# Strided heads' transposes moved into the second layer, batch 1's strided heads first, and the last output tile in halves

## The chip, the cores and the metric

The kernel runs on one core of a Trainium2 chip. A core has a matrix engine (TensorE, PE in the profile), a vector engine (VectorE, DVE), an activation engine (ScalarE, ACT), GpSimd (POOL) and SyncE (SP); the last two issue nearly all transfers here, which run on 16 shared DMA engines. TensorE's results go to PSUM, eight banks of 2 KB per partition, and are copied from there by DVE or ACT. The metric is the device time of one execution in microseconds, the median over runs.

## The reference

Two stages follow each other. The first is attention over 8 batches, 8 heads, 576 positions and a head size of 64. Heads 0 to 3 look at the last 32 positions, heads 4 to 7 at every fourth of the last 128:

```python
scores = scale * np.matmul(q, k.transpose(0, 1, 3, 2))
rel = pos[:, None] - pos[None, :]
mask_plain = (rel >= 0) & (rel < window)                # window 32
mask_dil = (rel >= 0) & (rel < window * dilation) & (rel % dilation == 0)   # dilation 4
scores = np.where(masks, scores, -1e9)
attn = exp(scores - max); attn = attn / (sum(attn) + 1e-9)
attn_out = np.matmul(attn, v)
```

The second is a two-layer network on the 4608 tokens (8 x 576) of 512 features, the heads side by side:

```python
h = x @ w_in                        # 512 -> 2048
g = h * (1.0 / (1.0 + np.exp(-h)))  # Silu
out = g @ w_out                     # 2048 -> 512, float32
```

## The kernel before

All matmuls are in float16 with sums in float32. The work of one batch has three parts.

Attention is done in two halves that the code calls z: z = 0 is the four plain heads, z = 1 the four strided heads, whose positions are sorted into four residue classes. One half of one batch goes through these steps:

- `load_qk` brings Q and K with positions on the partitions (tiles `n0`, `n1`; POOL issues the loads, eight per batch).
- `transpose` turns K (`which` = 1) or Q (0) on TensorE into two PSUM tiles `t`, 36 small transposes each for z = 0 and 12 each for z = 1; two copies bring them to SBUF, the first on DVE, the second on ACT (line 264 into `kT` and `qT`, line 273 into `kC` and `qC`). `transposes` does K and then Q.
- `scores` makes the score matmuls of 32 queries by 64 keys into PSUM tiles `s` and `ss` (72 matmuls for z = 0, 80 for z = 1), adds the mask on DVE (lines 414 and 423, tile `ms`) and takes the negative maximum (line 430, `nm`).
- `exps` runs Exp on ACT, one instruction per 64 keys with the maximum as bias and the sum taken out (line 458, 18 or 20 instructions per half). For batch 1's strided heads `shift` subtracts the maximum on DVE first (line 440), so that ACT needs one wide instruction per tile (line 452), and DVE makes the sums later (line 467).
- `normal` divides by the sums on DVE (lines 471 to 474, tile `pn`), `turn` transposes the result on TensorE (line 483), `turned` copies it out on DVE (line 491, `ptT`).
- `values` multiplies with V (lines 516, 570, 581; tiles `x`, `xs`), and `finish` copies the result on DVE into `xT`, the input of the network.

The first layer runs over 16 blocks f of the 2048 features: eight matmuls into a PSUM tile `h` (line 610) and a Silu on ACT into `gT` (line 618). Batch 0's first layer is done in two parts of the positions, two blocks at a time (lines 629 and 636). The second layer takes output tiles of 128 tokens, four for an even batch and five for an odd one (two batches make nine): 16 matmuls each (line 646) into a PSUM tile `o`, a copy on DVE into `ob` (line 654) and a transfer to the output by SP (line 656).

Exp and Silu are in different tables of ACT, which changes between them by a table load, once at the start of each first layer and once at its end.

PSUM is shared out as two tiles of two banks (`big`, for `h` and `o`) and four tiles of one bank (`ps`, for all else, given out in turn); a tile is free again when its copies are done.

The order of the work is written out by hand, and every engine keeps it. The main loop goes through the batches; for each, the first layer and then the second. Before each piece `plan(s)` puts out what `plan_of(b)` has listed for step s. Steps 0 to 15 are the blocks of the first layer, and from 16 on each step is four matmuls of the second layer, so 16 to 31 for an even batch and 16 to 35 for an odd one. For batch 0 the first part of the first layer has steps -16 to -1. Within one batch's first and second layer the plan thus places the attention of the next batch: scores of the plain heads in the second layer of the batch before the last, scores of the strided heads at step 9 of the first layer, exps at step 16, and the rest (`later`) at four given steps.

Of the kernel before, what the change touches and what calls it, by code (L numbers as in the profile page):

```python
# [14 lines left out]
P = 128  # L15
# [12 lines left out]
def kernel(  # L28
# [9 lines left out]
    nc = tc.nc  # L38
    B, H, S, D = q.shape
    DM, DFF = moe_w_in.shape  # L40
# [146 lines left out]
    def clear_v(b, engine):  # L187
# [13 lines left out]
        out=band[0:W], in_=band[0:W], compare_op=ALU.is_ge, fill=NEG,  # L201
# [3 lines left out]
        out=band[0:W], in_=band[0:W], compare_op=ALU.is_ge, fill=NEG,  # L205
# [432 lines left out]
    def layer2(b, plan):  # L638

        tiles = range(0, 4) if b % 2 == 0 else range(4, 9)  # L640
        for x, t in enumerate(tiles):
            o = big.tile([P, 2, 512], F32, tag="big", name=f"o_{b}_{t}")[:, 0]
            for f in range(NFF):
                if f % 4 == 0:
                    plan(NFF + 4 * x + f // 4)
                nc.tensor.matmul(  # L646
                    o,
                    gT[:, f, t * P : (t + 1) * P],
                    w_out16[:, f, :],
                    start=(f == 0),  # L650
                    stop=(f == NFF - 1),
                )
            ob = o32.tile([P, DM], F32, tag="o32", name=f"ob_{b}_{t}")
            nc.vector.tensor_copy(ob, o)  # L654
            row = (b // 2) * 2 * S + t * P
            nc.sync.dma_start(out=out[row : row + P, :], in_=ob)

    both = (nc.vector.tensor_copy, nc.scalar.copy)  # L660

    def transposes(at, b, z, step):
        for which in (1, 0):
            at(step, transpose, b, z, which, both)

    def later(at, b, z, steps):

        for hi in (0, 1):
            at(steps[hi], normal, b, z, hi)
        for fn in (turn, turned):  # L670
            for hi in (0, 1):
                at(steps[2], fn, b, z, hi)
        at(steps[3], values, b, z)
        at(steps[3], finish, b, z)

    def plan_of(b):
        ev = {}

        def at(s, fn, *args):
            ev.setdefault(s, []).append((fn, args))  # L680

        def all_exps(b, z):
            for hi in (0, 1):
                at(16, exps, b, z, hi)

        if b == 0:

            at(-15, normal, 0, 1, 1)
            at(-14, turn, 0, 1, 1)
            at(-14, turned, 0, 1, 1)  # L690
            at(-13, normal, 0, 0, 1)
            at(-12, values0, 1, 1)
            at(-12, finish0, 1, 1)
            at(-10, turn, 0, 0, 1)
            at(-10, turned, 0, 0, 1)
            at(-8, last_values, 0, 1, 1)
            at(-8, last_finish, 0, 1, 1)
            at(-7, values0, 0, 1)
            at(-7, finish0, 0, 1)
            at(-3, last_values, 0, 0, 1)  # L700
            at(-3, last_finish, 0, 0, 1)
            transposes(at, 1, 0, 1)
            at(5, scores, 1, 0)
            transposes(at, 1, 1, 8)
            at(10, load_qk, 3)
            at(10, load_v, 2)
            at(10, shift_v, 2, nc.gpsimd, (ALL,))
            at(12, scores, 1, 1)
            for hi in (0, 1):
                at(12, shift, 1, 1, hi)  # L710
            at(14, shift_v, 1, nc.sync, (ALL,))
            all_exps(1, 0)
            all_exps(1, 1)
            later(at, 1, 0, (20, 22, 25, 26))
            later(at, 1, 1, (25, 27, 29, 30))
        elif b == 1:
            at(16, load_v, 3)
            at(16, shift_v, 3, nc.gpsimd, (ALL,))
            transposes(at, 2, 0, 2)
            transposes(at, 2, 1, 9)  # L720
            transposes(at, 3, 0, 15)
            at(6, scores, 2, 0)
            at(17, load_qk, 4)
            at(12, scores, 2, 1)
            all_exps(2, 0)
            all_exps(2, 1)
            at(17, scores, 3, 0)
            at(18, exps, 3, 0, 0)
            at(18, exps, 3, 0, 1)
            later(at, 2, 0, (22, 24, 27, 28))  # L730
            later(at, 2, 1, (29, 31, 33, 34))
        else:
            if b + 2 < B:
                at(16, load_v, b + 2)
                at(16, shift_v, b + 2, nc.gpsimd, (ALL,))
            if b + 1 < B:
                transposes(at, b + 1, 1, 0)
                later(at, b + 1, 0, (0, 0, 4, 6))
                if b + 3 < B:
                    at(16, load_qk, b + 3)  # L740
            if b + 2 < B:
                transposes(at, b + 2, 0, 13)
                at(17, scores, b + 2, 0)
                at(18, exps, b + 2, 0, 0)
                at(18, exps, b + 2, 0, 1)
            if b + 1 < B:
                at(9, scores, b + 1, 1)
                all_exps(b + 1, 1)
                later(at, b + 1, 1, (22, 24, 27, 28))

        def plan(s):
            for fn, args in ev.pop(s, ()):
                fn(*args)

        return plan
# [36 lines left out]
    for b in range(B):  # L792
        plan = plan_of(b)
        if b == 0:
            for part in (0, 1):
                for f in range(0, NFF, 2):
                    plan(f - NFF * (1 - part))
                    plan(f - NFF * (1 - part) + 1)
                    layer1_part(f, part)
        else:  # L800
            for f in range(NFF):
                plan(f)
                layer1(b, f)
        layer2(b, plan)
        for s in range(NFF, 3 * NFF):
            plan(s)
# [30 lines left out]
```

## Time and profile before

| what | value |
|---|---|
| median of 3 runs | 343.28 us (342.47 to 344.01) |
| profiled execution, its own time | 343.56 us |
| span of its instructions | 341.8 us |
| mean granted TensorE clock | 0.993 |
| busy: TensorE, ACT, DVE, POOL | 314.5, 216.6, 180.5, 88.3 us |
| second layer, line 646 | 576 matmuls, 129.5 us |
| first layer, line 610 (batches 1 to 7) | 896 matmuls, 115.9 us |
| first layer of batch 0, line 629 | 128 matmuls, 20.8 us |

The span is from the first to the last instruction; the execution's own time has 1.8 us around it. Batch 0's first layer begins at 25.8 us and its second at 53.4, batch 1's first layer at 74.1 and its second at 94.1. From there two batches take about 77 us. The last matmul ends at 338.1 us.

How to read the lines that follow: in a row by time the columns are start, length (both us), engine, line, operation, the tile written and the tiles read, shapes, and how many instructions are merged; a bracket says how long the engine sat idle before it and what ended that. PEld is TensorE's loading of weights, which overlaps its matmuls. In a list of waits the numbers are the total in us, how often, and the longest. The granted clock is a share of TensorE's full speed.

### The profile page before, as it was taken

To read this page: it belongs to the slowest core of one execution; us is meant where nothing else is said; L and a number is where in the kernel's file an instruction comes from. 1 tells how busy PE (TensorE), PEld (TensorE's weight loads), DVE (VectorE), ACT (ScalarE), POOL (GpSimd) and SP (SyncE) were. 2 spreads that over 40 slices of the span, in tenths; PEclk is the share of its full clock that TensorE was granted. 3 is DMA by queue.
4 is the path that set the end of the run, shared out by engine and by line. 5 is a ranking of instruction groups with operands and counts; after the bars stand their busy time and mean duration, and the time that the engine had idled before them with its cause. 6 is when DMAs were issued, how large, how long until landed. Compare 5 with 4: busy or idle time off the path is not lost.

```text
span 341.8 us, 11965 instructions
## 1 busy us (share of the span) xinstructions
PE 314.5 (92%) x5216; PEld 204.4 (60%) x5216; DVE 180.5 (53%) x382; ACT 216.6 (63%) x746; POOL 88.3 (26%) x148
## 2 busy tenths in 40 slices
PE   4549799789999899998999899998999899999995
PEld 3437565457745577457755587457755577457642
DVE  7776337765658725765555535665556533440011
ACT  2693548516699856976699456976699456916400
POOL 8825746352500560047003530042000000000000
PEclk9999989999999999999999999999999999999999
DMA  6999999977802894079502980066002100110021
GB/s 83 166 219 205 193 195 213 210 136 100 133 22 82 125 138 78 35 118 172 79 28 80 190 134 2 34 117 115 2 17 80 63 2 2 61 63 2 0 86 70
DMA packets 45061, 32.90 MB, mean 96 GB/s; under 512 B 21872, under 2 KB 39536, under 8 KB 45008
## 3 DMA queue, kind: packets, MB, share of 16 engines
q0 software_dynamic: 38816, 21.74, 46.4%
q1 hardware_dynamic: 6192, 10.39, 8.6%
q8 instruction: 41, 0.67, 0.8%
q14 instruction: 12, 0.10, 0.1%
HBM read 37.75 MB, written 9.44 MB: 138 GB/s over the span
## 4 chain that ended last, share of the span: by engine, by line
PE 78%; ACT 9%; DMA 5%; DVE 3%; issue 2%; POOL 1%; SPq 0%; POOLq 0%
PE o L646 31%; PE h L610 30%; PE h L629 6%; ACT pe L458 4%; PE t L260 3%; PE x L516 2%; PE pt L483 2%; DMA vw<-in_v_dram 2%; ACT L618 2%; DMA vw<-vw 2%; DMA n<-in_k_dram 2%; PE s L306 1%; PE s L318 1%; DVE pn L474 1%; ACT gT L618 1%
## 5 line engine op out<-in xcount | busy, mean ns | idle before, releaser
L646 PE MATMUL o<-w_out,gT 128*128 128x512 f16 x576 | 129.5, 380 | 0.0
L610 PE MATMUL h<-xT,w_in 128*128 128x288 f16 x896 | 115.9, 287 | 4.5 <-ACT gT L618 4.5
L618 ACT ACTIVATE gT<-h 128x576 f16<-128x576 f32 x112 | 72.3, 650 | 64.3 <-PE h L610 63.5
L610 PEld LDWEIGHTS <-w_in 128*128 128x128 f16 x896 | 85.3, 98 | 27.5 <-issue 5.4
L458 ACT ACTIVATE pe<-ms,nm 128x64 f32<-128x64 f32 x284 | 94.3, 334 | 3.3 <-DVE nm L387 3.2
L646 PEld LDWEIGHTS <-gT 128*128 128x128 f16 x576 | 54.7, 98 | 61.7
L654 DVE COPY ob<-o 128x512 f32<-128x512 f32 x36 | 24.8, 689 | 61.2 <-PE o L646 61.2
L458 ACT ACTIVATION_READ_ACCUMULATOR pe<-ms,nm 128x1 f32 x284 | 53.2, 187 | 0.0
L414 DVE SCALAR_TENSOR_TENSOR ms<-s,mask 128x512 f32<-128x512 f32 x28 | 19.2, 686 | 40.3 <-PE ss L306 19.3
L127 POOL DMA_DIRECT2D vw<-in_v_dram x16 | 10.0, 630 | 94.0 <-PE x L516 94.0
L474 DVE TENSOR_TENSOR pn<-pe,r 128x640 f16<-128x640 f32 (+2 forms) x32 | 25.3, 792 | 1.1
L597 DVE CAST xT<-x 128x512 f16<-128x512 f32 x28 | 18.0, 685 | 12.0 <-PE xs L570 10.3
L430 DVE TENSOR_REDUCE nm<-ms 128x10 f32<-128x640 f32 (+1 forms) x28 | 22.0, 786 | 1.0
L629 PE MATMUL h<-xT,w_in 128*128 128x256 f16 (+1 forms) x128 | 20.8, 322 | 0.8 <-DVE xT L556 0.8
L491 DVE COPY ptT<-pt 128x640 f16<-128x640 f16 (+2 forms) x32 | 13.9, 469 | 13.8 <-PE pt L483 13.6
L636 ACT ACTIVATE gT<-h 128x512 f16<-128x512 f32 (+1 forms) x16 | 10.4, 650 | 15.5 <-PE h L629 15.4
L102 POOL DMA_DIRECT2D n<-in_q_dram x28 | 16.4, 598 | 12.5 <-DMA w_in<-in_moe_w_in_dram 6.4
L102 POOL DMA_DIRECT2D n<-in_k_dram x28 | 16.4, 594 | 11.4 <-DMA w_in<-in_moe_w_in_dram 3.9
L483 PE MATMUL pt<-ident,pn 128*128 128x128 f16 x152 | 12.7, 228 | 4.7 <-DVE pn L474 4.7
L629 PEld LDWEIGHTS <-w_in 128*128 128x128 f16 x128 | 13.2, 108 | 5.5 <-issue 0.8
L483 PEld LDWEIGHTS <-pn 128*128 128x128 f16 x152 | 10.4, 101 | 8.0 <-DVE pn L474 5.3
L273 ACT COPY kC<-t 128x576 f16<-128x576 f16 x7 | 4.5, 637 | 15.4 <-PE t L260 15.4
(79 smaller groups left out, 252.7 us busy)
## 6 DMA issues: line engine op xcount, KB each, us to landing
out_dram<-ob SPq DMA_DIRECT2D x36, 256.0 KB, 2.0
n<-in_k_dram POOLq DMA_DIRECT2D x28, 144.0 KB, 5.4
n<-in_q_dram POOLq DMA_DIRECT2D x28, 144.0 KB, 5.6
vw<-in_v_dram POOLq DMA_DIRECT2D x8, 288.0 KB, 6.2
vw<-in_v_dram POOLq DMA_DIRECT2D x16, 128.0 KB, 4.1
w_in<-in_moe_w_in_dram POOLq DMA_DIRECT2D x4, 512.0 KB, 11.6
w_out<-in_moe_w_out_dram POOLq DMA_DIRECT2D x4, 512.0 KB, 10.6
vw<-vw POOLq DMA_DIRECT2D x12, 128.0 KB, 3.3
```

Source lines behind the costliest of these rows:

```text
L102: nc.gpsimd.dma_start(out=qk[b, z, which][i * HF : i * HF + UPS[z]].rearrange("p h u d -> p h (u d)"), in_=src[b, h : h + 2].rearrange("h ...
L414: nc.vector.scalar_tensor_tensor(out=ms[:, 0:8].rearrange("p (n t) c -> p n (t c)", n=2), in0=s[hi].rearrange("p n t c -> p n (t c)"), sca ...
L430: nc.vector.tensor_reduce(out=nm[:, 0:w], in_=ms[:, 0:w], axis=AX.X, op=ALU.max, negate=True)
L458: nc.scalar.activation(pe[:, t, :], ms[:, t, :], AF.Exp, bias=nm[:, t : t + 1], accum_out=l[:, t : t + 1],)
L474: nc.vector.tensor_tensor(pn[:, 0:w], a["pe", z, hi][:, 0:w], r[:, 0:w, None].broadcast_to([P, w, KB]), ALU.mult)
L483: nc.tensor.transpose(t[:, i, :], a["pn", z, hi][:, 2 * i : 2 * i + 2].rearrange("p t c -> p (t c)"), ident)
L597: copy(a["xT"][:, 2 * z : 2 * z + 2, 0:NS].rearrange("d n (m e c) -> d n m e c", e=2, c=run)[:, :, :, e, :], a["x", z][e].rearrange("d n ( ...
L610: nc.tensor.matmul(h[:, half, 0:HS], w_in16[:, c, f * P : f * P + P], xT[:, c, half * HS : half * HS + HS], start=(c == 0), stop=(c == MC ...
L618: nc.scalar.activation(gT[:, f, s0 : s0 + S].rearrange("p (a c) -> p a c", a=2), h[:, :, 0:HS], AF.Silu)
L629: nc.tensor.matmul(h[:, i, 0 : c1 - c0], w_in16[:, c, (f + i) * P : (f + i + 1) * P], xT[:, c, c0:c1], start=(c == 0), stop=(c == MC - 1),)
L646: nc.tensor.matmul(o, gT[:, f, t * P : (t + 1) * P], w_out16[:, f, :], start=(f == 0), stop=(f == NFF - 1),)
L654: nc.vector.tensor_copy(ob, o)
```

## The change

Three things are changed in the order of the work, and nothing in what is computed.

The strided heads' transposes for batches 4 to 7 went out at step 0, ahead of a first layer. They now go out at step 30 of the second layer before it. Those for batch 3 went out at step 0 of batch 2 too; now K's go out at step 1 and Q's at step 3 of batch 2.

For batch 1, prepared during batch 0, the two halves change places. Strided heads: transposes at step -2 (before 8), scores and `shift` at 4 (before 12), `later` at 18, 20, 25, 26 (before 25, 27, 29, 30). Plain heads: transposes at 8 (before 1), scores at 14 (before 5), `later` at 22, 25, 28, 29 (before 20, 22, 25, 26). The exps of the strided heads now come first.

The very last output tile is copied and sent in two halves of 256 columns: the first copied by ACT and sent from ACT's queue, the second copied by DVE and sent from SP's. Before, DVE copied all 512 columns and SP sent them.

```diff
             ob = o32.tile([P, DM], F32, tag="o32", name=f"ob_{b}_{t}")
-            nc.vector.tensor_copy(ob, o)
             row = (b // 2) * 2 * S + t * P
-            nc.sync.dma_start(out=out[row : row + P, :], in_=ob)
+            if (b, t) == (B - 1, 8):
+                m = DM // 2
+                nc.scalar.copy(ob[:, 0:m], o[:, 0:m])
+                nc.scalar.dma_start(out=out[row : row + P, 0:m], in_=ob[:, 0:m])
+                nc.vector.tensor_copy(ob[:, m:DM], o[:, m:DM])
+                nc.sync.dma_start(out=out[row : row + P, m:DM], in_=ob[:, m:DM])
+            else:
+                nc.vector.tensor_copy(ob, o)
+                nc.sync.dma_start(out=out[row : row + P, :], in_=ob)
...
-            transposes(at, 1, 0, 1)
-            at(5, scores, 1, 0)
-            transposes(at, 1, 1, 8)
+            transposes(at, 1, 1, -2)
+            at(4, scores, 1, 1)
+            for hi in (0, 1):
+                at(4, shift, 1, 1, hi)
+            transposes(at, 1, 0, 8)
...
-            at(12, scores, 1, 1)
-            for hi in (0, 1):
-                at(12, shift, 1, 1, hi)
+            at(14, scores, 1, 0)
             at(14, shift_v, 1, nc.sync, (ALL,))
+            all_exps(1, 1)
             all_exps(1, 0)
-            all_exps(1, 1)
-            later(at, 1, 0, (20, 22, 25, 26))
-            later(at, 1, 1, (25, 27, 29, 30))
+            later(at, 1, 1, (18, 20, 25, 26))
+            later(at, 1, 0, (22, 25, 28, 29))
...
             if b + 1 < B:
-                transposes(at, b + 1, 1, 0)
+                if b == 2:
+                    for n in (0, 1):
+                        at(1 + 2 * n, transpose, 3, 1, 1 - n, both)
                 later(at, b + 1, 0, (0, 0, 4, 6))
...
+            if b + 2 < B:
+                transposes(at, b + 2, 1, 30)
```

## The prediction

> **What bounds the kernel now.** I read the busy table first, then the chain of waits, then who waited for whom on TensorE, then the order in time around each wait found.
>
> ```profile
> span 341.8 us, 11965 instructions
> PE 314.5 (92%) x5216; PEld 204.4 (60%) x5216; DVE 180.5 (53%) x382; ACT 216.6 (63%) x746; POOL 88.3 (26%) x148
> ...
> PE 78%; ACT 9%; DMA 5%; DVE 3%; issue 2%; POOL 1%; SPq 0%; POOLq 0%
> ```
> ```profile
> PE pt L483 <- DVE pn L474: 4.7, 4, 1.8
> PE h L610 <- ACT gT L618: 4.5, 5, 0.9
> PE s L306 <- issue: 2.4, 1, 2.4
> ```
>
> TensorE (PE) bounds it: 92% busy and 78% of the chain. Its work is only reordered, so time can come only from its waits. After the start (matmuls of the first layer from 25.8 us) these are, in order: 2.37 us at 40.8 put down to issue; 1.51 and 1.82 us in batch 0's second layer, for `pn` from VectorE (DVE); five of 0.90 us for ScalarE (ACT); 0.33 at 299.1.
>
> ```profile
> 152.00 0.77 PE L260 MATMUL t<-ident,n 48*128 48x48 f16 x48
> ...
> 152.54 0.64 ACT L273 COPY kC<-t 128x576 f16<-128x576 f16 x1 [1.94 <-PE t L260]
> ...
> 153.07 0.65 ACT L273 COPY qC<-t 128x576 f16<-128x576 f16 x1
> ...
> 153.74 1.28 ACT L618 ACT_TABLE_LOAD   x1
> ...
> 155.03 1.19 ACT L618 ACTIVATE gT<-h 128x576 f16<-128x576 f32 x2
> ...
> 155.73 2.12 PE L610 MATMUL h<-xT,w_in 128*128 128x288 f16 x16 [0.90 <-ACT gT L618]
> ```
>
> This is the start of batch 3, and those of batches 2, 4, 5 and 6 look the same. ACT had nothing to do for 1.94 us, then got two copies, and only then loaded the Silu table; TensorE, with two `h` buffers, ran out of them.
>
> ```profile
> 43.15 0.19 PE L306 MATMUL s<-kT,qT 64*32 64x64 f16 x1 [2.37 <-issue]
> ```
> ```profile
> 43.00:44.00 1.00, 0.85 (x9) 0.58 (x9) 0.62 (x2) 0.00 (x0) 0.00 (x0) 0.83 1.24 206
> 44.00:45.00 1.00, 1.00 (x6) 0.56 (x4) 0.97 (x3) 0.00 (x0) 0.56 (x1) 0.50 1.32 197
> ...
> 46.00:47.00 1.00, 1.00 (x5) 0.56 (x4) 0.00 (x0) 0.10 (x1) 0.00 (x0) 0.50 1.96 168
> 47.00:48.00 1.00, 1.00 (x51) 0.68 (x49) 0.21 (x1) 0.61 (x2) 0.50 (x1) 0.96 2.26 173
> ```
> ```profile
> q8 instruction: 1, 0.02, 5.5%
> ```
>
> Columns of the middle lines: stretch, its length, busy time of PE, PE's weight loads, DVE, ACT, POOL, then granted clock, DMA share, GB/s. The gap comes five score matmuls before the end of `scores(1, 0)`; then the clock is 0.5 until about 47.1. The 16 matmuls after the gap take 4.02 us where equal ones take 2.35: another 1.67 lost. The last line is DMA between 40.8 and 41.9 us: a 16 KB instruction packet, started at 40.87, done at 41.84; 1.31 us later TensorE goes on. There are 41 such packets for about 10,450 TensorE instructions, one per 256. Counting from the gap back, the previous boundary was crossed at 37.2; so the packet lay 3.6 us in full queues (DMA is over 90% busy until 60 us). The neighbours agree: crossed 43.15 and started 47.24, crossed 50.6 and started 54.35. Later, with emptier queues, a packet starts within 1 us and is at least 3.5 us early.
>
> **The change part by part.** The sum is made against the profiled execution, 343.56 us (span 341.8 and 1.8 around it); the median of the three runs, 343.28, is 0.28 below.
>
> *Starts of batches 2 to 6.* For batches 3 to 6 the 48 transposes and their four copies go to step 30 of the second layer before. Take the one at 152: step 30 lies 8 matmuls (1.7 us) before its end, so transposes at about 150.3. Exps hold ACT until 150.6; then 0.64 + 0.65 for `kC` and `qC` to 152.1, and the table load of 1.28 to 153.4. The first `h` still starts at 152.7 (transposes merely come earlier) and is done at 153.75: the table is there 0.35 before it is wanted. After odd batches there are 5 us instead of 1.7. Buffers at step 30: the four `ps` tiles were last `x` and `xs`, copied out by 149.65 and 149.91. DVE now has `kC`, `qC` (0.75 each, to 152.1) before `ob`, which is ready at 152.7 anyway; the normals behind end earlier than before. Batch 2's start instead gets batch 3's transposes after `h` 0 and `h` 2: ACT has 0.33 us free per `h` (0.65 of 0.98), so each copy (0.64) delays one Silu by 0.3, which two buffers absorb; DVE does the normals (2.3 us) first, `kC` by 3.7 and `qC` by 4.9 after the start, turns come at 5. So 5 x 0.90 = 4.5 go. Cutting one more run of matmuls costs TensorE about 0.1 (24 `h` matmuls between two switches 3.05, 24 of an unbroken run 2.94), six times, 0.5 rounded: **-4.0**. Bounds: -4.5 (switches free) and -2.5 (ACT late by half the stall after each).
>
> *Batch 1's order in the first layer of batch 0.* Transposes (48 at step -2, 72 at step 8), scores (80 at 4, 72 at 14) and copies are the same ones, next to the same matmuls; the strided K and Q of batch 1 were issued at 15.4 to 17.6 us, and the slowest such load takes 15.5, so they are there at 36.1. DVE's `shift` now follows the first scores: 5.2 us of work from 41 to 46.2; the plain transposes' copies behind it (2 x 0.75) end at 47.7, wanted by `scores(1, 0)` at 48.0. What does move is the count of instructions. The boundary crossed at 37.2 is now crossed in the transposes about 0.6 earlier (36.7), so its block is there at 36.7 + 3.6 + 1.0 + 1.3 = 42.6. The next boundary falls, by the order of the built program, no longer inside the scores but three matmuls into `h` of f = 6, reached at 42.5: a wait of 0.15 in place of 2.37, too short for the clock row to repeat (the 1.82 gap at 68 left it at 1.00). The block after that, asked for at 42.65 with 4.1 of queue, is there at 49.0 and wanted in `scores(1, 0)` at 48.4: 0.6 of new wait (before, the slow clock hid it). So 2.37 + 1.67 - 0.75 = 3.3, less 0.1 for one more switch: **-3.2**. Bounds: -4.0 (no fetch wait left) and +1.0 (old wait and clock loss stay, and the 0.6 - 1.0 comes on top). I take the row-based value because three packets agree on 3.6 to 4.1.
>
> The Trainium skill, "TensorE: Matmul & The Clock Gate", Part 1, speaks against the clock part: it has the clock fall only after an idle window of about 3.4 us. Here 2.37 us were enough; by the page that 1.67 would not belong to the gap and this term would be -1.5, the sum 1.7 less.
>
> *Batch 0's second layer.* It starts at L (53.36 before) and takes 20.75 to the next `h` at 74.11. Now: ACT's table is there at L+2.2, two shifted exps (0.67 each) to 3.5, 18 plain ones (0.33) to 9.5. DVE in its order: normal 2.1 to L+5.1; `ob` 0.69 to 5.8; normal to 7.9; plain normal 1.2 to 9.1; `ob` to 9.8; both `ptT` 0.9 to 10.7; the last normal to 11.9; finish 1.65 to 13.55. TensorE turns at 7.95, does 4 matmuls to 9.5, then values wait for `ptT` until 10.75: 1.25 us, new. `ob` 14.45, `ptT` 15.3, values at 15.35: 0.05. The two `pn` waits (1.51 + 1.82) go, since `pn` is there 0 and 1.8 early. 3.33 - 1.3, less 0.1: **-1.9**. Bounds: -3.2 and -0.5 (DVE 0.7 later at each of the two turns). On POOL nothing is moved; SP's four moves of V for batch 1 keep their place (landed by 56.3).
>
> *Last tile.* The 0.69 copy becomes 0.4 on ACT (between 128x256 f16 at 0.372 and Silu of 512 at 0.600) and 0.42 on DVE (128x256 CAST). In the built program the DVE half waits for the ACT half, so data is out at about 0.87: 0.18 later. The last transfer moves 0.8 us for 256 KB (packets 339.6 to 340.4); half of it saves up to 0.4, and ACT's half is away before. ACT has no queued work then. **-0.1**, between -0.4 and +0.4.
>
> The Trainium skill, "PSUM — Partial Sum Buffer", on bank collisions, says why: two engines may not touch one bank and quadrant at once, so halves of one bank go in turn. Had they run together, by the rows 0.27 would be saved instead of 0.18 lost.
>
> Sum: -4.0 - 3.2 - 1.9 - 0.1 = -9.2, so **334.4 us**.
>
> **The rivals.** (1) The fetch wait stays: if the block comes no earlier, or the next one starves `scores(1, 0)` for over 2 us, the half clock follows again. For it: no profile shows that queue at 36.7, and the margin is tenths. The term goes from -3.2 to about 0: 337.6. (2) ACT is not freed: at step 30 it is late after the even batches (2 of 5 starts, margin 0.35), or the turn after `h` 3 of batch 2 waits. Then up to 2.0 of the 4.0 stay: 336.4. (3) Slower: the step-30 transposes wait for DVE's finish copies, in the middle of the bound engine's stream, four times. They have 0.25 to 0.5 us of margin and DVE sat idle 0.93 before the like finish at 113.25, which speaks against it; it would have to cost (9.2 + 1.7)/4 = 2.7 us at each for a loss of 0.5%, say 346. (4) The change does nothing that counts: a later wait in each first layer takes back the 0.90 and the fetch wait stays; 341 to 343. Against it: no other TensorE wait of those batches is in the trace, and pn is ready about 1 us before its turn.
>
> **How the numbers follow.** Forecast 0.62 (332.8 to 336 by its own bounds), rival 1 0.18, rival 2 0.10, rival 3 0.04, rival 4 0.06. Under 0.5%, 1.7 us, a measurement of this kernel can't tell from no change (the runs shown spread over 1.5). Rivals 1 and 2 together reach 339.5, so 332.5 to 339.5 leaves out rivals 3 and 4 and some of the edges, under 0.2. Faster is the forecast, 1, 2 and a little of 4: 0.90; same most of 4: 0.05; slower 0.05.
>
> **What would show it.** Right: no `PE h L610 <- ACT gT L618` wait and the table load ahead of the first `h`; an issue gap under 1 us near 42 and 48 with the clock at 1.00; one wait `x <- ptT` of about 1.2 in place of two for `pn`; the stretch from the first `h` of batch 1 on shorter by 4. Wrong: the clock at 0.5 anywhere after 26 us, waits of `t L260` for DVE, or DVE's half copy waiting long at the end.

## The result and the profile after

| what | before | after |
|---|---|---|
| median of 4 runs each | 343.33 us (342.47 to 344.01) | 333.95 us (332.95 to 334.36) |
| ratio of the times | | 0.9724, 95% interval 0.9693 to 0.9754 |
| profiled execution | 343.56 us, span 341.8 | 332.95 us, span 331.2 |
| mean granted clock | 0.993 | 1.000 |

The changed kernel is 2.8% faster: 9.4 us by the medians, 10.6 by the two profiled executions. The one of after is the lowest of its four runs, which accounts for the 1 us between the two figures.

The page of after, its span, its busy table and the engines' shares of the chain that ended last:

```profile
span 331.2 us, 11975 instructions
...
PE 312.4 (94%) x5216; PEld 204.4 (62%) x5216; DVE 181.0 (55%) x382; ACT 217.4 (66%) x747; POOL 88.2 (27%) x148
...
PE 85%; DMA 4%; DVE 3%; ACT 3%; POOL 2%; issue 2%; SPq 0%; POOLq 0%; ACTq 0%
```

TensorE has the same 5216 matmuls and is busy 2.1 us less, most of it because the stretch at half clock is gone. Its share of the chain rises from 78 to 85%, and ACT's falls from 9 to 3%. From the list of who waited for whom on TensorE in after (total in us, how often, longest):

```profile
PE pt L483 <- DVE pn L474: 1.7, 2, 1.3
...
PE x L516 <- DVE ptT L491: 0.7, 2, 0.5
PE s L306 <- issue: 0.7, 1, 0.7
...
PE x L516 <- issue: 0.5, 1, 0.5
```

There is no line `h L610 <- ACT gT L618` any more; before it had 4.5 us in five waits. Of the four waits for `pn`, 4.7 us, two are left: one lies ahead of the change's first step and the other, 0.33 us, near 289. The new ones in order of time, from the timeline of TensorE:

```profile
48.57 0.49 PE L306 MATMUL s<-kT,qT 64*32 64x64 f16 x42 [0.71 <-issue]
```
```profile
60.02 0.19 PE L516 MATMUL x<-ptT,vw 64*64 64x32 f16 x1 [0.51 <-DVE ptT L491]
60.41 0.70 PE L516 MATMUL x<-ptT,vw 64*64 64x32 f16 x63 [0.21 <-DVE ptT L491]
65.89 0.30 PE L516 MATMUL x<-ptT,vw 64*64 64x32 f16 x14 [0.51 <-issue]
```

The start of batch 3, the counterpart of the stretch at 152 shown for before:

```profile
144.10 0.77 PE L260 MATMUL t<-ident,n 48*128 48x48 f16 x48
...
144.64 0.64 ACT L273 COPY kC<-t 128x576 f16<-128x576 f16 x1 [0.22 <-PE t L260]
...
145.17 0.65 ACT L273 COPY qC<-t 128x576 f16<-128x576 f16 x1
...
145.84 1.28 ACT L618 ACT_TABLE_LOAD   x1
...
146.54 1.51 PE L610 MATMUL h<-xT,w_in 128*128 128x288 f16 x11
...
147.72 0.65 ACT L618 ACTIVATE gT<-h 128x576 f16<-128x576 f32 x1 [0.60 <-PE h L610]
```

The last bracket has turned round: ACT now waits 0.60 us for TensorE's `h`, where TensorE had waited 0.90 us for ACT.

To see where the time went, I cut the span of each profiled execution in four, at instructions that every kernel has: A, from the span's start to the 49th `h` matmul of batch 0 (a bit before the first step that the change touches); B, from there to the first `h` of batch 1 (the rest of batch 0's two layers); C, from there to the end of the last matmul; D, what follows it.

| kernel | A | B | C | D |
|---|---|---|---|---|
| before | 35.16 | 38.95 | 263.93 | 3.74 |
| after | 35.33 | 33.45 | 258.87 | 3.53 |
| difference | +0.17 | -5.50 | -5.06 | -0.21 |

B splits at the start of batch 0's second layer into 18.20 + 20.75 before and 14.82 + 18.63 after: -3.38 and -2.12. A holds nothing that was changed; over the profiled executions below it takes 34.4 to 36.8 us, and 37.3 in experiment 4, so single times differ by a microsecond or two without any cause in the change, and B and C are what to compare. Most of that spread goes with the clock, though its column reads 1.00 there. In after, eight first-layer matmuls of batch 0 take at first as long as sixteen do later:

```profile
27.80 1.91 PE L629 MATMUL h<-xT,w_in 128*128 128x256 f16 x8
...
33.31 1.92 PE L629 MATMUL h<-xT,w_in 128*128 128x256 f16 x16
```

The rate doubles at 30.8 us, where the trace's record of the clock begins; the column counts the time ahead of that record as full. In the three executions where this comes earliest, at 28.4 to 28.9 us, A is 34.4 to 34.7; in the four where it comes latest, at 32.2 to 33.1, A is 36.6 to 37.3.

### The profile page after: what moved, and what is told of

Same layout as the page of the kernel before. It is cut to its first block, busy times and chain, and to the rows that moved or that the text cites. A ratio compares the mean times of both kernels' runs of the same rounds, so it can differ in the third digit from the quotient of the medians.

```text
span 331.2 us, 11975 instructions
## 1 busy us (share of the span) xinstructions
PE 312.4 (94%) x5216; PEld 204.4 (62%) x5216; DVE 181.0 (55%) x382; ACT 217.4 (66%) x747; POOL 88.2 (27%) x148
## 4 chain that ended last, share of the span: by engine, by line
PE 85%; DMA 4%; DVE 3%; ACT 3%; POOL 2%; issue 2%; SPq 0%; POOLq 0%; ACTq 0%
PE h L610 34%; PE o L646 33%; PE h L629 5%; PE t L260 3%; PE x L516 3%; PE pt L483 2%; DMA vw<-in_v_dram 2%; ACT pe L458 2%; DMA vw<-vw 2%; POOL n L119 1%; PE s L318 1%; PE s L306 1%; DVE pn L474 1%; PE ss L318 1%; PE xs L581 1%
## 5 line engine op out<-in xcount | busy, mean ns | idle before, releaser
L618 ACT ACTIVATE gT<-h 128x576 f16<-128x576 f32 x112 | 72.8, 650 | 71.2 <-PE h L610 70.4
L610 PE MATMUL h<-xT,w_in 128*128 128x288 f16 x896 | 115.4, 286 | 0.0
L610 PEld LDWEIGHTS <-w_in 128*128 128x128 f16 x896 | 85.7, 98 | 23.0
L662 DVE COPY ob<-o 128x512 f32<-128x512 f32 x35 | 24.1, 689 | 52.5 <-PE o L646 52.5
L474 DVE TENSOR_TENSOR pn<-pe,r 128x640 f16<-128x640 f32 (+2 forms) x32 | 25.3, 792 | 1.1
L629 PE MATMUL h<-xT,w_in 128*128 128x256 f16 (+1 forms) x128 | 19.3, 306 | 0.8 <-DVE xT L556 0.8
L491 DVE COPY ptT<-pt 128x640 f16<-128x640 f16 (+2 forms) x32 | 13.9, 469 | 10.5 <-PE pt L483 10.3
L516 PEld LDWEIGHTS <-vw 64*64 64x64 f16 x896 | 8.7, 108 | 6.5 <-issue 6.4
```

The costliest lines, as they stand in the source:

```text
L474: nc.vector.tensor_tensor(pn[:, 0:w], a["pe", z, hi][:, 0:w], r[:, 0:w, None].broadcast_to([P, w, KB]), ALU.mult)
L516: nc.tensor.matmul(dst, w, p, start=True, stop=True)
L610: nc.tensor.matmul(h[:, half, 0:HS], w_in16[:, c, f * P : f * P + P], xT[:, c, half * HS : half * HS + HS], start=(c == 0), stop=(c == MC ...
L618: nc.scalar.activation(gT[:, f, s0 : s0 + S].rearrange("p (a c) -> p a c", a=2), h[:, :, 0:HS], AF.Silu)
L629: nc.tensor.matmul(h[:, i, 0 : c1 - c0], w_in16[:, c, (f + i) * P : (f + i + 1) * P], xT[:, c, c0:c1], start=(c == 0), stop=(c == MC - 1),)
```

## The experiments

My theory: three separate gains, which add up: at the starts, where ACT's table load comes earlier; in batch 0's first layer, where an instruction packet had queued behind loads and the clock had then fallen; and in its second layer. The rivals: that the wait put down to issue belongs to the scores at that place and not to a packet; that the parts need each other; that another price than the waits shown lies behind the starts.

**1. The starts alone.** Before, with only the transposes of batches 3 to 7 moved:

```diff
-                transposes(at, b + 1, 1, 0)
+                if b == 2:
+                    for n in (0, 1):
+                        at(1 + 2 * n, transpose, 3, 1, 1 - n, both)
...
+            if b + 2 < B:
+                transposes(at, b + 2, 1, 30)
```

> The kernel before with one part of the change: the strided heads' transposes of batches 3 to 7 moved (step 30 of the second layer before; steps 1 and 3 for batch 3). Theory (ACT's two copies ahead of the Silu table load starve TensorE at five starts): each of batches 3 to 6 gives back about 1.07 us and batch 2 about 0.85, as in the trace after, so 338.2 us; batch 0's stretch is untouched, with its 2.37 us issue gap and the half clock. Rival (the gain of the starts needs the earlier order of batch 1, or a later wait takes it back): under 2.5 us of gain, 341 or more.

Measured: 338.49 us, ratio 0.9853 (0.9835 to 0.9871), so -5.1 against the 343.61 of before on that chip. A 35.16, B 38.36, C 259.31. Of the 5.06 that C lost in the whole change, 4.62 are here; the other 0.44 is lost in batch 1's second layer, 21.37 in place of after's 20.94, where a wait of 0.24 put down to issue ends at 94.95 (more on it in experiment 12). The fetch wait stayed, and the clock fell. TensorE's timeline, then a stretch of 1 us (busy PE, PEld, DVE, ACT, POOL, then clock, DMA share, GB/s):

```profile
42.91 0.19 PE L306 MATMUL s<-kT,qT 64*32 64x64 f16 x1 [2.12 <-issue]
```
```profile
44.00:45.00 1.00, 1.00 (x6) 0.58 (x5) 0.84 (x2) 0.47 (x1) 0.00 (x0) 0.53 1.38 194
```

The first layers of batches 3 to 5 take 18.81, where before has 19.87 to 19.88, and that of batch 6, which has fewer transposes in it, 17.95 in place of 19.01; the second layers with the moved transposes in them take 16.98 and 20.41 to 20.43, where before has 16.97 and 20.40 to 20.42. Breaking a run of `o` matmuls cost 0.01, not the 0.1 that I had charged.

**2. Batch 1's order alone.** Before, with the other main part:

```diff
-            transposes(at, 1, 0, 1)
-            at(5, scores, 1, 0)
-            transposes(at, 1, 1, 8)
+            transposes(at, 1, 1, -2)
+            at(4, scores, 1, 1)
+            for hi in (0, 1):
+                at(4, shift, 1, 1, hi)
+            transposes(at, 1, 0, 8)
...
-            at(12, scores, 1, 1)
-            for hi in (0, 1):
-                at(12, shift, 1, 1, hi)
+            at(14, scores, 1, 0)
...
+            all_exps(1, 1)
             all_exps(1, 0)
-            all_exps(1, 1)
-            later(at, 1, 0, (20, 22, 25, 26))
-            later(at, 1, 1, (25, 27, 29, 30))
+            later(at, 1, 1, (18, 20, 25, 26))
+            later(at, 1, 0, (22, 25, 28, 29))
```

> The kernel before with the other part alone: batch 1's strided heads first, spread over batch 0's first layer. Theory: 25.8 to the first matmul of the second layer 24.6 us instead of 27.6, the second layer of batch 0 18.6 instead of 20.75, the five 0.90 us waits for ACT stay; 343.3 - 5.1 = 338.2 us. Rival (the waits for pn and the issue gap only come together with work that e1 moves): under 3 us of gain.

Measured: 338.79 us, ratio 0.9879 (0.984 to 0.9918), -4.8. A 35.16, B 33.68, C 263.95: all of it in B, -5.27, and nothing in C. Its list of waits on TensorE:

```profile
PE h L610 <- ACT gT L618: 4.5, 5, 0.9
...
PE x L516 <- issue: 1.0, 1, 1.0
...
PE x L516 <- DVE ptT L491: 0.7, 2, 0.5
...
PE s L306 <- issue: 0.5, 1, 0.5
```

The five starts wait as before, and the small new waits of after are here too. The two parts, -5.1 and -4.8, make 9.9; the whole took 9.4 off in the result above and 10.3 in experiment 11, so within that spread they do not depend on each other. One of the four runs, the slowest with 340.96 us, has a mean granted clock of 0.995 where the others have 1.000; a stretch of 3.4 us at half clock makes that of 339 us. It left no trace, but it says that the new order does not keep the clock up in every execution.

**3. A lighter DMA load ahead of the gap.** Before, with three of the four loads of `w_out` left out and the first quarter used for all blocks:

```diff
-                    w_out16[:, f, :],
+                    w_out16[:, f % 4, :],
...
-    for c in range(4):
-        load_w_out(c)
+    load_w_out(0)
```

> The kernel before with only the first quarter of w_out loaded, and that quarter used for all sixteen blocks (the other three quarters of w_out are left out of the sum): 1.5 MB less in the transfer queues at 33 to 45 us, the same instructions on TensorE. Theory (the 2.37 us gap is an instruction block that lies in full queues): the block starts within 1.5 us of the crossing at 37.2 instead of 3.6, the gap is under 0.5 us and the clock stays at 1.00; 343.3 - 4.0 = 339.3 us. Rival (the gap belongs to the score matmuls or to a buffer): gap and clock as before, 343.

Measured: 341.11 us, ratio 0.9927 (0.991 to 0.9944). The gap fell to a third and the clock stayed at 1.00, from the timeline of TensorE:

```profile
41.26 0.19 PE L306 MATMUL s<-kT,qT 64*32 64x64 f16 x1 [0.80 <-issue]
47.73 0.39 PE L318 MATMUL s<-kC,qC 64*32 64x64 f16 x29 [0.47 <-issue]
```

The boundary was crossed at 36.90 (37.23 before); the packet started 1.99 us later, at 38.89, in place of 3.64. That is the queue: the same program with the same boundaries waited 1.6 less when 1.5 MB less was asked for. It did not go under 0.5 as I had said, since 2 us of queue are left, and the next packet now met a wait of 0.47 (it started 3.77 after its request). The total came out 1.8 above what I expected: 0.3 of gap beyond what I had allowed, 0.47 that was new, and 0.39 more in C (264.32), 0.37 of it in batch 1's second layer. That last has a wait of 0.18 put down to issue in it, which ends at 92.43 at the same matmul as the one of experiment 1. The rest is not explained.

**4. The boundaries moved, the load left.** Before, with 16 matmuls of zeros ahead of everything on TensorE:

```diff
+    zero = cpool.tile([P, 2 * W], F16, name="zero")
+    nc.vector.memset(zero, 0.0)
+    pad = ps.tile([P, W], F32, tag="ps", name="pad")
+    for _ in range(16):
+        nc.tensor.matmul(pad[0:W], zero[0:W, 0:W], zero[0:W, W : 2 * W], start=True, stop=True)
```

> The kernel before with 16 small matmuls of a zero tile put ahead of TensorE's first transpose, where it waits over 4 us for data: 32 instructions more, nothing else moved. Theory (the gap stands at a boundary of 256 instructions): a gap of 2.2 to 2.6 us comes 16 matmuls earlier in the scores, 21 matmuls before their end instead of 5; time 342.5 to 344. Rival (a wait of that matmul for a buffer or an engine): the gap stays five matmuls before the end.

Measured in a single run: 345.61 us, which I had put at 342.5 to 344. The timeline of TensorE:

```profile
43.86 0.26 PE L306 MATMUL s<-kT,qT 64*32 64x64 f16 x17 [1.11 <-issue]
```
```profile
95.04 0.22 PE L260 MATMUL t<-ident,n 64*64 64x64 f16 x2 [2.25 <-issue]
```

The place of the gap is right to the instruction: 21 score matmuls before the end of `scores(1, 0)` instead of 5, sixteen earlier. So the gap belongs to a count of instructions and not to a tile. Its length is not right: 1.11, with no fall of the clock, since the packet started 2.29 after its request. And a wait of 2.25 appeared at 95, where before has none. The granted clock there, in two stretches of 1 us from the same kernel:

```profile
94.00:95.00 1.00, 0.00 (x0) 0.00 (x0) 0.00 (x0) 0.00 (x0) 0.00 (x0) 1.00 0.21 35
95.00:96.00 1.00, 0.96 (x9) 0.77 (x9) 0.74 (x1) 0.64 (x1) 0.00 (x0) 1.00 0.03 6
```

This wait makes C 266.40, 2.47 more than before's, while B is 36.46, 2.49 less; A has the late start of the full clock in it (37.26). Sixteen matmuls more, and other boundaries come to lie at dense places: one cannot move one boundary alone.

**5. The lighter load in after.** The edit of experiment 3 in the changed kernel.

> The changed kernel with only the first quarter of w_out loaded and used for all blocks (three quarters of w_out left out of the sum), the twin of the same edit on the kernel before (341.1 us). Theory: the change's part in batch 0's first layer (2.95 us of 10.6 in the traces) was mostly the fetch gap and its half clock, which that edit already took from the kernel before; so this gains little here, 333.3 us, and the two twins differ by 7.5 to 8 instead of 9.4. Rival (that part is the order of the work itself): the twins differ by 9.4, 331.7 us.

Measured: 331.70 us, ratio to before 0.9648 (0.9624 to 0.9672). By the medians the two light kernels stand 9.4 apart, as the full ones do: the rival's number, against mine of 7.5 to 8. The stretches say otherwise. B is 36.22 and 32.22, so 4.00 apart where the full kernels are 5.50 apart; the waits put down to issue are gone in this kernel (1.27 of them were left in its twin). What fills the total up is C, 5.44 apart, with the 0.39 of experiment 3 in it, where a fetch wait stands too. So the prediction of the total failed, and the reading by stretches supports the theory; it is the weaker of my tests.

**6. All starts by steps 1 and 3.** After, with K's transposes at step 1 and Q's at step 3 of each first layer, as batch 2 has them:

```diff
-                if b == 2:
-                    for n in (0, 1):
-                        at(1 + 2 * n, transpose, 3, 1, 1 - n, both)
+                for n in (0, 1):
+                    at(1 + 2 * n, transpose, b + 1, 1, 1 - n, both)
...
-            if b + 2 < B:
-                transposes(at, b + 2, 1, 30)
```

> The changed kernel with the strided transposes of batches 4 to 7 at steps 1 and 3 of the first layer, as it has them for batch 3, instead of step 30 of the second layer. Theory (the 0.90 us came from two copies ahead of the Silu table load, wherever else they go): no wait of h for gT comes back; one more cut per batch costs about 0.2 as at batch 2, 4 x 0.2 = 0.9, so 334.8 us. Rival (the room that ACT has in the second layer is what counts): waits of 0.3 to 0.9 at the starts of batches 3 to 6, 336 to 338 us.

Measured: 335.0 us, ratio 0.9745 (0.9715 to 0.9775). The start of batch 3 in its timeline:

```profile
145.63 1.28 ACT L618 ACT_TABLE_LOAD   x1
146.92 1.14 PE L610 MATMUL h<-xT,w_in 128*128 128x288 f16 x8
147.99 0.47 PE L260 MATMUL t<-ident,n 48*128 48x48 f16 x24
...
148.65 0.63 ACT L273 COPY kC<-t 128x576 f16<-128x576 f16 x1
```

The table load comes first here too, and no `h` waits for ACT. A second layer and the first one after it take 16.17 + 19.83 = 36.00 in this kernel and 16.98 + 18.81 = 35.79 in after: 0.21 for two short runs of transposes among `h` matmuls, which I had put at 0.1 each. Whatever takes the transposes from ahead of the first `h` gets the gain; the place decides 0.2.

**7. The last tile whole.** After, with the old copy and transfer of the last tile.

> The changed kernel with the last tile copied whole by DVE and sent whole by SP, as before. Theory: from the last matmul's end to the end of the span 3.72 us as in the trace of before instead of 3.53, 334.1 us, not told apart from 333.95 by the times. Rival (the halves cost, since DVE's half waits for ACT's): the end is shorter here, by up to 0.2.

Measured: 333.25 us, ratio 0.969 (0.966 to 0.9719): by time not told apart from after. D is 3.75 and 3.53. After's end, then that of this kernel:

```profile
327.69 0.37 ACT L657 COPY ob<-o 128x256 f32<-128x256 f32 x1 [16.62 <-PE o L646]
...
328.09 0.42 DVE L659 COPY ob<-o 128x256 f32<-128x256 f32 x1 [3.17 <-ACT ob L657]
328.55 0.33 SPq L660 DMA_DIRECT2D out_dram<-ob  x1
```
```profile
328.08 0.69 DVE L655 COPY ob<-o 128x512 f32<-128x512 f32 x1 [2.76 <-PE o L646]
328.80 0.33 SPq L656 DMA_DIRECT2D out_dram<-ob  x1
```

The halves go one after the other, DVE's released by ACT's; the last matmuls end at 327.65 and 328.04. So the last transfer is issued 0.90 after the last matmul instead of 0.76, but carries half as much: 0.22 saved.

**8. The loads held back.** After, with the loads of Q and K for batches 2 and 3 and of V for batch 2 behind a tiny copy on POOL that reads a late result (`gate`), so that POOL issues them later:

```diff
-            at(10, load_qk, 3)
-            at(10, load_v, 2)
-            at(10, shift_v, 2, nc.gpsimd, (ALL,))
+            at(14, gate, gT[0:1, 12, S - 1 : S])
+            at(14, load_qk, 2)
+            at(27, gate, att(1)["xT"][0:1, 3, NS - 1 : NS])
+            at(27, load_qk, 3)
+            at(27, load_v, 2)
+            at(27, shift_v, 2, nc.gpsimd, (ALL,))
...
-    load_qk(2)
```

> The changed kernel, with loads that nobody needs soon kept out of the queues: POOL issues batch 2's Q and K only after the Silu of batch 0's blocks 12 and 13 (it first copies one value of gT), and batch 3's Q and K and batch 2's V only after batch 1's strided heads are finished (one value of xT). Same instructions on TensorE. Theory (what is left of batch 0's TensorE waits is instruction blocks in full queues): the waits of 0.71 at 48 us and 0.51 at 65.5 fall under 0.2 each; 332.9 us. Rival (those waits have another cause, or the loads put off come too late and stall batch 1): 334 or more.

Measured: 333.08 us, ratio 0.9681 (0.9655 to 0.9708). B is 32.47, 0.98 less than after's; of the waits put down to issue 0.19 is left, and the 0.53 and 0.21 for `ptT` stand as before. By the time alone it can't be told from after.

**9. The same, with more room for `ptT`.** Experiment 8 with the second gate and its loads at step 28 and

```diff
-            later(at, 1, 1, (18, 20, 25, 26))
-            later(at, 1, 0, (22, 25, 28, 29))
+            later(at, 1, 1, (18, 20, 25, 27))
+            later(at, 1, 0, (22, 25, 29, 30))
```

> The changed kernel with the loads of Q and K for batches 2 and 3 and of V for batch 2 held back until the first layer of batch 0 has reached f = 12, or step 28, and with the last values of batch 1's strided heads one step later (27), the plain heads' last steps at 29 and 30. Theory (the two waits for instruction blocks, 0.71 and 0.51, come from packets that lie behind these loads, and the 0.51 for ptT from a turn that is one step too close): none of the three waits remains, batch 0's second layer takes 17.6 to 18.2 instead of 18.63 and its first layer about 24.1; time about 332.6, 1.0 to 1.5 under the changed kernel on the same chip. Rival (the gated loads only move the waits to batch 1, where they are wanted): the sum stays within 0.3 of the changed kernel's, and a new wait over 0.5 stands in batch 1's first or second layer.

Measured: 331.74 us (330.46 to 332.55), ratio to before 0.9641 (0.9607 to 0.9676). Beside it on the same chip after took 333.41 (332.96 to 334.22, experiment 11): the six runs of each do not overlap, and the gain is 1.7 us. B is 31.55, its second layer 16.85 where I expected 17.6 to 18.2; C is 258.86, so nothing came back later. One wait was not removed, at 49.1 us, from the list of waits on TensorE:

```profile
PE s L306 <- issue: 0.6, 1, 0.6
```

The other packet shows what the held-back loads do. After, then this kernel, in the stretch in which the boundary is crossed (60.60 in after, 61.72 here), columns as above:

```profile
60.00:62.00 2.00, 1.77 (x83) 1.37 (x83) 1.93 (x5) 0.99 (x1) 0.63 (x2) 1.00 1.25 208
```
```profile
60.00:62.00 2.00, 2.00 (x62) 1.03 (x63) 1.93 (x7) 1.98 (x7) 0.00 (x0) 1.00 0.20 77
```

With a DMA share over 1 the packet starts 3.01 after its request and TensorE waits 0.51; with 0.20 it starts after 0.97 and nothing waits.

**10. One step later.** After, with the transposes of batches 4 to 7 at the last step of each second layer:

```diff
-                transposes(at, b + 2, 1, 30)
+                transposes(at, b + 2, 1, 31 if b % 2 == 0 else 35)
```

> The changed kernel with the transposes of batches 4 to 7 one step later: step 31 after even batches, step 35 after odd ones (the last step of each second layer). Theory (the start is right as long as the table load is over when the second h is done; at step 30 it was there 0.6 early): the copies come 0.86 later after even batches, so Silu starts up to 0.3 late, which the second h buffer takes; no wait of h for gT over 0.1, starts as in the changed kernel within 0.1 each, time within 0.4 of it. After odd batches the old step 30 left 5 us, the new one 0.9 less than the even ones had, so the same holds. Rival (no reserve: TensorE follows ACT's lateness at once): up to 0.3 to 0.9 at each of four starts, 1.2 to 3.6 in all, and waits of h for gT come back.

Measured: 335.22 us (333.07 to 336.5), ratio 0.9743 (0.9698 to 0.9787). The start of batch 3 in its timeline:

```profile
145.79 3.42 PE L610 MATMUL h<-xT,w_in 128*128 128x288 f16 x25
145.95 1.28 ACT L618 ACT_TABLE_LOAD   x1
...
147.25 1.38 ACT L618 ACTIVATE gT<-h 128x576 f16<-128x576 f32 x2
...
147.95 1.07 PEld L610 LDWEIGHTS <-w_in 128*128 128x128 f16 x9 [0.20 <-issue]
```

Silu now follows the table load without a break, and a pause of 0.20, put down to issue, comes before the weights of the third `h` block. The first layers of batches 3 to 5 take 19.00 in place of 18.81, that of batch 6 18.14 in place of 17.95. So step 30's reserve is the 0.60 shown, a step costs 0.86 of it, and of the 0.26 beyond it 0.19 reaches TensorE. My expectation, that the second `h` buffer takes it, was wrong. In the profiled execution C is 259.63, 0.76 over after's. The median is 1.8 over; that is more than the trace shows.

**11. After once more,** on the same chip as experiments 9 and 10.

> The changed kernel once more, as the yardstick for the two kernels beside it on the same chip: 333.0 to 334.4, with the same waits, 0.71 and 0.51 put down to issue and 0.51 for ptT. If the waits put down to issue are chance of one execution, they differ here by more than 0.3; if they follow from the order of the program and the loads, they agree within 0.1.

Measured: 333.41 us (332.96 to 334.22). The waits did not repeat within 0.1: 1.13 and 1.02 in place of 0.71 and 0.51. The later one:

```profile
65.89 0.30 PE L516 MATMUL x<-ptT,vw 64*64 64x32 f16 x14 [1.02 <-issue]
```

By the mark I had set, a difference over 0.3, the size of these waits is chance of one execution. Their place is not: the one near 48 us stands before the same matmul in all seven profiled executions with this order and these loads, the later one in six of the seven. The later one ends at 65.89, as in the first profile, and batch 1's first `h` starts at 68.79 (68.78). But A is 34.44 here, 0.89 shorter, and B 34.35, 0.90 longer: TensorE came early and waited the time off. The packet was asked for at 60.13 and started at 63.61; in the first profile it was asked for at 60.60 and started at 63.60. So it does not start a fixed time after its request. That it waits for the queues ahead of it fits experiment 9 but is not shown here: at 63.60 the DMA share was still over 1, and loads that POOL issued at 58.3 to 59.5 landed only at 64.9 to 65.4. Nor is an early TensorE always held up: in experiment 10 A is 34.51, 0.82 shorter, and B only 0.08 longer.

**12. One step later after even batches only.**

```diff
-                transposes(at, b + 2, 1, 30)
+                transposes(at, b + 2, 1, 31 if b % 2 == 0 else 30)
```

> The changed kernel with the transposes at step 31 after the even batches only (for batches 4 and 6), and at step 30 after odd ones. The kernel with all four a step later showed 0.19 to 0.20 lost at each start in its trace, but a median 1.8 over the changed kernel. Theory (a start costs the part of ACT's lateness that passes 0.6, here 0.26, and nothing else; the rest of the 1.8 is spread of the beginning of an execution): two starts lose 0.19 each, 333.4 + 0.4 = 333.8, and the two others take 18.81 as in the changed kernel. Rival (the later step has a price that the profiled execution does not show): about half of 1.8, 334.3 or more.

Measured: 333.61 us (333.17 to 334.46), ratio 0.9701 (0.967 to 0.9732). The first layers of batches 3 to 6 take 19.00, 18.81, 19.00 and 17.95, where after has 18.81 three times and 17.95: the price goes with the step, 0.19 each. C is 259.90, with a wait put down to issue in batch 1's second layer that after does not have:

```profile
89.99 0.20 PE L306 MATMUL ss<-kT,qT 64*32 64x64 f16 x1 [0.42 <-issue]
```

It stands before TensorE's 1629th matmul, as do the waits of 0.24 in experiment 1, 0.18 in experiment 3 and 2.25 in experiment 4 (its sixteen added ones counted), so all four belong to one boundary. That second layer takes 21.57 here, 0.64 over after's 20.93; in experiments 1 and 3 it took 0.43 and 0.37 more than in the kernels that they are compared with, so such a wait costs some 0.2 more than it shows. The time is near the theory's 333.8 and under the rival's 334.3. Why the median of experiment 10 lay 1 us higher than its 0.76 is open; the spread of A told above is enough to do it, but its other runs left no trace.

## Why the prediction was right

The forecast was 334.4 within 332.5 to 339.5; the median is 333.95. Its four terms against the profiled pair:

| term | predicted (bounds) | measured |
|---|---|---|
| starts of batches 2 to 6 | -4.0 (-4.5 to -2.5) | -5.06 |
| batch 1's order, first layer | -3.2 (-4.0 to +1.0) | -3.38 |
| batch 0's second layer | -1.9 (-3.2 to -0.5) | -2.12 |
| last tile | -0.1 (-0.4 to +0.4) | -0.21 |
| ahead of the change | 0 | +0.17 |
| sum | -9.2 | -10.60 |

*The starts.* The mechanism was right: the table load ahead of the first `h`, no wait in any of the five, ACT ready 0.60 early (predicted 0.35), and experiment 1 has the gain alone, but for the 0.44 told there. The size was outside its bounds, and two steps of the sum are to blame. "So 5 x 0.90 = 4.5 go" took the wait that the profile shows for its price. In an unbroken run of first-layer matmuls one starts every 0.123 us while each row is some 0.28 long, so rows overlap. In before the 17th `h` of batch 3 starts 3.03 after the first, in after 1.96: the pause cost 1.07, and 0.90 is only what lies between the end of one row and the start of the next. The other step is "Cutting one more run of matmuls costs TensorE about 0.1 ... six times, 0.5 rounded": moved into the second layer, the transposes cost 0.01 (experiment 1), and only the split at batch 2 cost something, 0.23. So 4 x 1.07 + 0.84 = 5.1.

*The fetch wait.* The row-based time of the packet held: boundary at 36.75 (predicted 36.7), packet started 3.26 later, and row f = 6, reached at 42.52 (42.5), waited not at all (0.15). The next packet, put at 0.6 of wait, cost 0.71, and 1.13 in the repeat. The clock stayed at 1.00 from 30.8 us to the last matmul (the half rate ahead of that is in both kernels), and the 1.67 went with the gap. That the gap is a packet in a queue, and not something in `scores`, is shown by experiments 3 and 4: less DMA load shortens it in place, sixteen matmuls more move it by sixteen. Rival 1 did not happen, but the repeat shows why it deserved its 0.18: this wait depends on when TensorE arrives, and it ranged from 0.48 to 1.13 in the seven profiled executions that share this order and these loads (after's two and experiments 2, 6, 7, 10 and 12). In none of them did the clock fall; in the slowest run of experiment 2, by its mean, it did.

The rule weighed in the prediction, from the Trainium skill's "TensorE: Matmul & The Clock Gate", Part 1, says that the clock falls after an idle window of about 3.4 us, and that the window runs freely. The runs split it. After pauses of 2.37 (before) and 2.12 (experiment 1) the clock was 0.5; after 2.25 in experiment 4 it was not. In before it fell at 43.7, 0.5 after the pause's end, and in experiment 1 at 44.1, 1.1 after it; both times it stayed down 3.4 us, to 47.1 and 47.5. The length of the window and its free running agree with that; that a whole window must be idle does not.

Where the windows lie can be worked out. In before the clock's record begins at 30.01, where the matmuls' rate doubles, and the fall at 43.66 comes 13.65 later, four times the 3.41 that the clock then stays down; in experiment 1 it is 30.40 and 44.05, 13.65 again. Counted so, each of the two pauses (40.78 to 43.15 and 40.79 to 42.91) lies inside one window, and TensorE was idle for 0.69 and 0.62 of it. In experiment 4, counted from 33.07, a window ends at 94.51 and cuts the pause (92.79 to 95.04) in two, which leaves that window 0.50 idle. In before the window from 67.56 to 70.97, with the 1.82 wait for `pn` in it, is 0.53 idle and the clock stays. So in these traces an idle share of 0.62 was enough and one of 0.53 was not; two falls are few to rest this on.

By the page the term would have been 1.9 short of the measured -3.38, so counting the 1.67 as the gap's was right for the profiled pair. The times of other runs show less of it: in four of the 38 runs of before beside the experiments the mean clock is 1.000, so it did not fall, and their median is 343.26 against 343.73 of the other 34. Experiments 3 and 4 show what can take its place: with the clock up, the next packet brings a wait of 0.47 and 0.53.

*Batch 0's second layer.* Both waits for `pn` went. The new wait for `ptT`, put at 1.25, was 0.51 + 0.21, and a wait that was not foreseen came with it: 0.51 put down to issue, for the packet asked for at 60.60. The two errors cancel (1.3 predicted, 1.23 measured), which is luck. The step that failed is the count of boundaries: I followed the instruction blocks to the end of the first layer and not into the second. In before two boundaries fall among the values' matmuls as well, but 7.2 us apart (64.54 and 71.73), with the 1.82 wait for `pn` between them; without that wait TensorE had 4.8 us of work from one to the next, and the packet, started 3.0 after its request in queues that were still full, came too late. Experiment 9 takes both waits out and shortens this layer by 1.8, 0.55 more than they show. Experiment 8, where only the wait of 0.51 put down to issue is gone, takes 17.94 for it, 0.69 less than after: here too a wait costs some 0.2 more than the idle time shown.

*The last tile.* Right in its parts: DVE's half waited for ACT's and was copied out 0.86 after the last matmul (0.87); the smaller last transfer gave a little more than that lost.

*Rivals 2 and 3* could be looked for in the trace: no wait of `h` for `gT` and none of the step-30 transposes for DVE. Experiment 10 shows how near rival 2 was: 0.86 later, and ACT is late. *Rival 4* would have needed a wait later in each first layer; C has none.

One reading of the working was wrong. Later packets are not all "at least 3.5 us early": in before the one asked for at 89.01 started at 92.22 and was done at 93.37, 1.7 before its instructions began at 95.09, and TensorE has needed 1.2 to 1.7 after a packet's end wherever it waited. That is the boundary at which experiments 1, 3, 4 and 12 wait.

The sum was 1.4 too small against the profiled execution, 1.06 of it in the starts. That the median lies closer to 334.4 than the sum deserved is luck: after's profiled execution is 1 us under its median.

## What to carry to other kernels

A wait that ends a run of pipelined matmuls costs more than the idle time beside it: compare the starts of the same instruction with and without it. This program has a boundary every 256 TensorE instructions, where the next block must have been fetched; count where they fall, above all among short matmuls while the DMA queues are full, because there TensorE waited for the fetch. Holding back loads that are wanted much later, with one step more of room for `ptT`, was worth 1.7 us here. When work is moved away from a phase change of ACT, read how early the table then stands ready: that reserve (0.60 here) is the distance to losing the gain again.

## What the runs showed of the hardware

- A 16 KB instruction packet for TensorE, taken to be asked for when the boundary before is crossed, started 0.9 to 1.7 us after that with the queues half empty (61.77 to 62.62 in experiment 8, 49.72 to 51.43 in experiment 9), and up to 4.4 under full ones (83.27 to 87.64 in experiment 12); where TensorE waited for it, it went on 1.2 to 1.7 us after the packet's end. The Trainium skill's "Runtime: NRT & Kernel Launch", "Instruction fetch mechanics", has the next block fetched while the current one runs and the crossing mostly hidden; where 256 instructions last under some 6 us and the DMA share is about 1, the runs show 0.2 to 2.4 us that are not.
- Such a packet can leave at the same time although it was asked for 0.47 us earlier (experiment 11); there a faster stretch ahead of it gained nothing, in experiment 10 it did.
- Half clock of 3.4 us followed pauses of 2.12 and 2.37 us, not one of 2.25 us. Counted in windows of 3.41 us from the clock's first change, idle shares of 0.62 and 0.69 brought it, 0.50 and 0.53 did not.
- In every profiled execution batch 0's first matmuls of the first layer (from 25.3 to 27.2 us on) ran at half rate until 28.4 to 33.1 us, and the granted clock's column does not show it.
- Breaking a run of `o` matmuls (128 rows by 512 columns) for 48 transposes cost 0.01 us, splitting a run of `h` matmuls for twice 24 transposes 0.21 to 0.23.
